# A layernorm, S5 recurrence and gated feed-forward kernel: outputs in the gate's buffers, one chunk's skip term on VectorE, and a reordered start

**Chip and metric.** One core of a Trainium2 chip. The time is the device time in microseconds (us) of one execution. "Span" is the time from the first to the last instruction in the profile; a timed execution is 1.73 to 1.86 us longer than its span in every kernel here but one (`skip_only`, 2.12 to 2.17).

## The reference

Types: bf16 in and out; L = 2048 tokens, D = 448, F = 1792.

```python
x  = A_x                                            # 1 x 2048 x 448
xn = (x - mean) / sqrt(var + 1e-5)                  # layernorm over D, no gain
Bu = xn @ B_bar^T                                   # complex, 448 states
h_t = Lam_bar * h_(t-1) + Bu_t                      # one recurrence over all tokens
s  = 2 * Re(h @ C^T) + xn * Dskip                   # "y" and the "skip"
g  = silu((silu(xn @ w_gate) * (xn @ w_up)) @ w_down)
out = x + s * g
```

## The kernel before

Tokens are worked on in four chunks (q = 0 to 3) of 512, each of four tiles (j) of 128. Per chunk: the two wide products (banks `gp`, `up`), their evacuation and product into `Vt`; `hd = Vt @ Wd` and the gate `sg = silu(hd)`; the inputs of the recurrence (`pb` banks), the scans on VectorE; `y` from the states; then the output. VectorE's scans of the next chunk run as "background" steps between its other work, so that whatever holds VectorE up early also delays everything behind it. The "root" is 1/sqrt(var) of a chunk, formed on GpSimd (`act_root`); `rcol` is a power that GpSimd forms from VectorE's `zr`, for the scans; the "iota" is GpSimd's count of the tokens (`count_tokens`). The parts that the change touches (cuts marked `# ...`):

```python
    def power(out, base, exponent):                 # GpSimd: e ** z, and 1/sqrt(var)
        powers.append(lambda: nc.gpsimd.tensor_tensor(out=out, in0=base, in1=exponent, op=ALU.pow))

    def tell(mm):                                   # a notice: a no-operation on GpSimd's queue
        told = nc.gpsimd.nop(nofuse=True)           # that waits for the matmul mm
        tc.add_manual_dep(told.ins, mm.ins.name, SYNC, reason="share")
        return told.ins.name

    def told_of(mm, notice):                        # matmul mm waits for the notice
        tc.add_manual_dep(mm.ins, notice, SYNC, reason="other half")

    def sums(q, pairs, between=None):               # two products at once, half the rows each;
        left = []                                   # the halves are exchanged after `tell`
        for share, first in ((0, True), (1, False)):
            for n, two in enumerate(pairs):
                # ... matmuls; the second share's first one waits: told_of(mm, left[n])
                if first:
                    left.append(tell(mm))
            if first:
                run_power()                         # a waiting pow goes onto GpSimd's queue here
            if first and between:
                between()

    def act_root(q):                                # 1/sqrt(var) of a chunk, on GpSimd
        # ... tensor_scalar vep <- sums ; tensor_tensor rstd <- vep ** -0.5 ; off_of <- off_of * rstd

    def down(q, j):
        # ... 14 matmuls into hd
        sg = work.tile([P, D], BF16, name="sg", bufs=TQ)
        nc.scalar.activation(sg[:], hd, ACT.Silu)
        return sg

    SKIPS = [(q, j) for q in (1, 2, 3) for j in range(TQ)][:-1]   # tiles whose skip VectorE adds

    def out_sum(q, j, k0=0, k1=KT):
        # ... seven matmuls into y, and where (q, j) is not in SKIPS also the skip term:
                nc.tensor.matmul(y[:, s + half : s + P], lhsT=xT[:, n, m * P : (m + 1) * P],
                                 rhs=Dd[:, n, half:P], start=False, stop=False)

    def finish(q, j, y, sg, eng=nc.sync, c0=0, c1=D):
        # ...
        if (q, j) in SKIPS:
            nc.vector.tensor_tensor(out=t[:], in0=y, in1=skip[q][:, j, c0:c1], op=ALU.add)
            y = t[:]
        nc.vector.tensor_tensor(out=t[:], in0=y, in1=sg[:, c0:c1], op=ALU.mult)
        ob = work.tile([P, c1 - c0], BF16, name="ob", **of)       # two buffers
        nc.vector.tensor_tensor(out=ob[:], in0=t[:], in1=x_all[:, m, c0:c1], op=ALU.add)
        eng.dma_start(out=out2d[m * P : (m + 1) * P, c0:c1], in_=ob[:])

    sg = downs(0, 1.8, {...})                       # 1.8 us of background per tile
    bg.finish(0)
    turned_norms(8, 9, 10, 11)                      # four token transposes on SyncE's queue
    outs(0, sg)                                     # and behind them the four output transfers
    sg = downs(1, 2.4, { ...
        2: act_sums((14, 15), 1) + [on(act_root, 3)],
    })
    drive(2, 4.8)
    gu(2, bg, 2.4)
    bg.finish(1)
    turned_norms(12, 13, 14, 15)
    outs(1, sg)
```

Of the kernel before, what the change touches and what calls it, by code (L numbers as in the profile page):

```python
# [44 lines left out]
def kernel(  # L45
# [187 lines left out]

    def ln_stats(n):
        st = work.tile([P, nc.vector.BN_STATS_DIM], F32, name="st")
        nc.vector.bn_stats(out=st[:], in_=x_all[:, n, :])
        nc.vector.bn_aggr(out=mv[:, n, :], in_=st[:])
        nc.vector.tensor_scalar(
            out=vep[:, n : n + 1], in0=mv[:, n, 1:2], scalar1=1e-5, scalar2=None, op0=ALU.add
        )  # L240
# [202 lines left out]

    def sums(q, pairs, between=None):

# [3 lines left out]
        for share, first in ((0, True), (1, False)):  # L449
            for n, two in enumerate(pairs):  # L450
                for m in range(4 - share):
                    for half in range(2):
                        out, w, (c0, c1) = two[half ^ share]
                        d, h = HALVES[half ^ share][share][m]
                        mm = nc.tensor.matmul(  # L455
                            out, lhsT=w[h, d, :], rhs=xT[h, d, q * W + c0 : q * W + c1],
                            start=(first and m == 0), stop=(not first and m == 3 - share),
                        )
                        if not first and m == 0:
                            told_of(mm, left[n])  # L460
                if first:
                    left.append(tell(mm))
            if first:
                run_power()
            if first and between:
                between()

# [88 lines left out]

    def gu_matmuls(q, f0, banks, *cols, **kw):

        cols = cols * (len(banks) if len(cols) == 1 else 1)
        sums(q, [  # L560
            [(to[:, c[0] : c[1]], w[:, :, block(f0 + n)], c) for to, w in zip(two, (Wg, Wu))]
            for n, (two, c) in enumerate(zip(banks, cols))
        ], **kw)

    def gu(q, bg, budget, hooks={}, begun={}):
# [3 lines left out]
        for f0 in range(0, NF, GRP):  # L569
# [3 lines left out]
            for i in range(0, n, 2):  # L573
# [3 lines left out]
                else:  # L577
                    banks = gu_banks()
                    gu_matmuls(q, fi, banks, (0, W))
                for j, (gp_, up_) in enumerate(banks):  # L580
# [12 lines left out]
    def down(q, j):  # L593

        hd = bank("hd")[:, 0:D]
        for fi in range(NF):
# [3 lines left out]
            )  # L600
        sg = work.tile([P, D], BF16, name="sg", bufs=TQ)
        nc.scalar.activation(sg[:], hd, ACT.Silu)  # L602
        return sg

    skip = {}
    SKIPS = [(q, j) for q in (1, 2, 3) for j in range(TQ)][:-1]

    def skips(q):

        skip[q] = work.tile([P, TQ, D], BF16, name="skip", tag="nz")  # L610
        for j in range(TQ):
            for c0, c1, x0 in ((0, KF * P, 0), (KF * P, D, KF * P + R)):
                nc.vector.tensor_tensor(
# [24 lines left out]
    def finish(q, j, y, sg, eng=nc.sync, c0=0, c1=D):  # L638
# [3 lines left out]
        if (q, j) in SKIPS:  # L642
            nc.vector.tensor_tensor(out=t[:], in0=y, in1=skip[q][:, j, c0:c1], op=ALU.add)
            y = t[:]
        nc.vector.tensor_tensor(out=t[:], in0=y, in1=sg[:, c0:c1], op=ALU.mult)  # L645
        of = dict(tag="scr_a") if c1 - c0 < D else {}
        ob = work.tile([P, c1 - c0], BF16, name="ob", **of)
        nc.vector.tensor_tensor(out=ob[:], in0=t[:], in1=x_all[:, m, c0:c1], op=ALU.add)  # L648
        eng.dma_start(out=out2d[m * P : (m + 1) * P, c0:c1], in_=ob[:])

# [10 lines left out]
    for n in range(2):  # L661
        ln_norm(n)
        ln_evacuate(n, ln_transpose(n), nc.scalar)
        warm(1 + n)
    for n in range(2, TQ):
        ln_stats(n)
        ln_root(n, n + 1)
    run_power()
    powers.append(count_tokens)

    def second_tokens():
        ln_evacuate(2, ln_transpose(2), nc.scalar)
        t = ln_transpose(3)
        tv = params_row(t)
        ln_evacuate(3, t, nc.vector)
        nc.scalar.activation(pcol[:], tv, ACT.Copy)
        power(dtv[:], euler[:], pcol[:, 0:KT, 0])

    CW = W // 2
    first, third = gu_banks(), gu_banks(1)  # L680
    gu_matmuls(0, 0, first, (0, CW))
    for n in range(2, TQ):
        ln_norm(n)
    gu_matmuls(0, 2, third, (0, CW), between=second_tokens)

    def first_pair():
        gu_matmuls(0, 0, first, (CW, W))
        return first

    def second_pair():  # L690
        banks = third + gu_banks(1)
        gu_matmuls(0, 2, banks, (CW, W), (0, W))
        return banks
# [67 lines left out]
    def act_sums(ns, squares):  # L761
# [3 lines left out]
    drive(1, 4.0)  # L765
    sg = downs(0, 1.8, {
        0: cw(2)[0] + cw(3)[0] + act_sums((8, 9), 0),
        1: act_sums((10, 11), 0) + [act_means] + act_sums((8, 9), 1) + cw(2)[1] + cw(3)[1],
        2: act_sums((10, 11), 1) + [on(act_root, 2), on(skips, 1)],
    })  # L770
# [3 lines left out]
    sg = downs(1, 2.4, {  # L774
        0: act_sums((12, 13, 14), 0) + [on(skips, 2)],
        1: act_sums((15,), 0) + [act_means] + act_sums((12, 13), 1),
        2: act_sums((14, 15), 1) + [on(act_root, 3)],
    })
    drive(2, 4.8)
    gu(2, bg, 2.4)  # L780
    bg.finish(1)
    turned_norms(12, 13, 14, 15)
    outs(1, sg)
    sg = downs(2, 2.4, {1: [on(skips, 3)]})
    drive(3, 4.8)
# [38 lines left out]
```

## Time and profile before

| | before |
|---|---|
| median of three timed runs (range) | 187.49 us (187.25 to 187.87) |
| the profiled run: time, span | 186.79 us, 185.0 us |
| TensorE busy | 177.9 us, 96% |
| longest wait of TensorE | 1.3 us, for Vt of the third chunk |
| longest idle of VectorE in the middle | 7.68 us, for an output transfer |

How to read the lines of the profile, here and in the prediction: a line of a timeline has start, duration, engine, line, operation, output <- inputs, sizes and count, and in brackets how long the engine stood idle before it and what ended that. A line of waits has who waited, for what, and then us in total, times, longest. "PEld" is TensorE's loading of weights, DVE VectorE, ACT ScalarE, POOL GpSimd, SP SyncE; a "q" behind the name means the engine's instruction queue.

The profile page cuts the span into 40 slices of 4.6 us and gives each engine's busy share in tenths. VectorE in the kernel before:

```profile
DVE  4649799999999999902999999999999999999583
```

The "02" in the middle is 78.6 to 87.9 us: VectorE does next to nothing there, the wait for the output tile. Everything between it and the tail is 9, so the lost time is not made up. The chain that ended last, summed by engine:

```profile
PE 67%; DVE 25%; DMA 3%; issue 2%; ACT 1%; POOL 0%; SPq 0%; DVEq 0%
```

A quarter of the path to the end runs through VectorE and a little through the DMA, although TensorE is busy 96% of the time.

### The profile page before, as it was taken

What the parts mean: (1) busy time and instruction counts of PE and PEld (TensorE: products, weight loads), DVE (VectorE), ACT (ScalarE), POOL (GpSimd) and SP (SyncE); (2) the same over time, 40 slices, a digit from 0 to 9 for tenths busy, and PEclk for the clock granted to TensorE, in tenths of its full rate; (3) what the DMA queues carried; (4) which work ended last, traced back from release to release, by engine and by line L of the source; (5) the groups of instructions that cost most, each with busy time, mean ns of one, the idle gap of its engine ahead of it and who ended that gap; (6) DMA issues with size and microseconds to landing.
All of it is one profiled execution on the core that took longest, in us unless ns stands there. A gap on an engine that the chain in (4) does not pass through costs nothing.

```text
span 185.0 us, 3723 instructions
## 1 busy us (share of the span) xinstructions
PE 177.9 (96%) x1449; PEld 87.8 (47%) x1449; DVE 160.1 (87%) x254; ACT 120.2 (65%) x247; POOL 13.4 (7%) x25
## 2 busy tenths in 40 slices
PE   7899999999999999999999999979999999999991
PEld 3574444544444555555454444535454444455551
DVE  4649799999999999902999999999999999999583
ACT  3247879997789999498499556962259696512110
POOL 7332200000000000600300000000000000000000
PEclk9999999999999999999999999999999999999999
DMA  5899655979200000043100000042100000001111
GB/s 160 209 277 338 124 94 112 132 167 377 101 0 0 5 0 0 0 86 81 50 2 4 2 0 4 0 82 70 62 4 0 0 4 0 0 4 50 50 50 50
DMA packets 26129, 12.71 MB, mean 69 GB/s; under 512 B 16000, under 2 KB 26112, under 8 KB 26112
## 3 DMA queue, kind: packets, MB, share of 16 engines
q1 hardware_dynamic: 24896, 12.06, 25.3%
q10 hardware_dynamic: 1088, 0.41, 0.8%
q8 instruction: 11, 0.18, 0.4%
q14 instruction: 6, 0.05, 0.1%
q0 software_dynamic: 128, 0.00, 0.0%
HBM read 7.23 MB, written 1.84 MB: 49 GB/s over the span
## 4 chain that ended last, share of the span: by engine, by line
PE 67%; DVE 25%; DMA 3%; issue 2%; ACT 1%; POOL 0%; SPq 0%; DVEq 0%
PE gp L455 20%; PE hd L597 16%; PE up L455 15%; PE pb L455 9%; PE y L626 7%; DVE bu_re L527 5%; DVE bu_im L527 4%; DVE tmp L521 2%; DVE Vt L589 2%; DVE ob L648 2%; DMA out_dram<-ob 2%; DVE t L645 2%; DVE H_im L521 2%; DVE ere L521 1%; DMA x_all<-in_A_x_dram 1%
## 5 line engine op out<-in xcount | busy, mean ns | idle before, releaser
L455 PE MATMUL gp<-xT,Wg 64*128 64x512 bf16 (+1 forms) x413 | 85.8, 365 | 0.4 <-ACT xT L304 0.3
L455 PE MATMUL up<-xT,Wu 64*128 64x512 bf16 (+1 forms) x413 | 85.8, 365 | 0.0
L455 PEld LDWEIGHTS <-Wg 64*128 64x128 bf16 x413 | 38.5, 94 | 25.1 <-issue 0.4
L455 PEld LDWEIGHTS <-Wu 64*128 64x128 bf16 x413 | 38.4, 94 | 19.7 <-POOLq L437 0.5
L581 ACT ACTIVATE gs<-gp 128x512 bf16<-128x512 f32 x56 | 33.7, 604 | 19.6 <-PE gp L455 11.7
L597 PE MATMUL hd<-Wd,Vt 128*128 128x448 bf16 x224 | 43.4, 353 | 1.3 <-DVE Vt L589 1.3
L585 ACT ACTIVATE us<-up 128x512 bf16<-128x512 f32 x54 | 32.9, 609 | 0.0
L597 PEld LDWEIGHTS <-Vt 128*128 128x128 bf16 x224 | 21.8, 98 | 22.0 <-DVE Vt L589 1.7
L602 ACT ACTIVATE sg<-hd 128x448 bf16<-128x448 f32 x16 | 8.6, 538 | 25.2 <-PE hd L597 20.6
L455 PE MATMUL pb<-xT,BT 64*128 64x512 bf16 (+1 forms) x224 | 21.9, 349 | 0.0
L648 DVE TENSOR_TENSOR ob<-t,x_all 128x448 bf16<-128x448 f32 (+2 forms) x17 | 10.2, 597 | 8.2 <-DMA out_dram<-ob 7.7
L589 DVE TENSOR_TENSOR Vt<-gs,us 128x2048 bf16<-128x2048 bf16 (+1 forms) x16 | 17.2, 1079 | 0.0
L455 PEld LDWEIGHTS <-BT 64*128 64x128 bf16 x224 | 10.7, 94 | 11.4 <-issue 0.7
L626 PE MATMUL y<-C,H_re 128*128 128x448 bf16 (+2 forms) x68 | 15.7, 342 | 0.0
L527 DVE TENSOR_TENSOR_SCAN bu_re<-rcol,H_re,ere 128x512 bf16<-128x512 f32 x12 | 14.9, 1262 | 0.1
L488 ACT ACTIVATE bu_re<-pb 128x512 bf16<-128x512 f32 (+1 forms) x20 | 10.1, 537 | 2.7 <-PE pb L455 2.6
L626 PE MATMUL y<-C,H_im 128*128 128x448 bf16 (+2 forms) x51 | 11.9, 342 | 0.0
L498 ACT ACTIVATE bu_im<-bu_re 64x512 bf16<-64x512 bf16 x16 | 10.0, 628 | 2.1 <-DVE bu_re L527 1.8
L527 DVE TENSOR_TENSOR_SCAN bu_im<-rcol,H_im,eim 128x512 bf16<-128x512 f32 x9 | 11.4, 1262 | 0.0
L287 ACT ACTIVATE xn<-x_all,off_of,rstd 128x384 bf16<-128x384 bf16 (+1 forms) x16 | 8.1, 588 | 2.8 <-POOL off_of L281 2.8
L521 DVE TENSOR_TENSOR tmp<-bu_im,ST 128x2048 bf16<-128x2048 bf16 x8 | 9.7, 1218 | 0.0
L626 PEld LDWEIGHTS <-H_re 128*128 128x128 bf16 x68 | 6.4, 98 | 6.1 <-issue 0.4
(98 smaller groups left out, 174.5 us busy)
## 6 DMA issues: line engine op xcount, KB each, us to landing
out_dram<-ob SPq DMA_DIRECT2D x15, 112.0 KB, 1.7
Wd<-in_B_w_down_dram SPq DMA_DIRECT2D x1, 1568.0 KB, 9.0
x_all<-in_A_x_dram SPq DMA_DIRECT2D x1, 896.0 KB, 5.5
Wg<-in_B_w_gate_dram SPq DMA_DIRECT2D x2, 384.0 KB, 7.0
Wu<-in_B_w_up_dram SPq DMA_DIRECT2D x2, 384.0 KB, 7.6
x_all<-in_A_x_dram SPq DMA_DIRECT2D x1, 448.0 KB, 5.7
Wg<-in_B_w_gate_dram SPq DMA_DIRECT2D x1, 288.0 KB, 3.1
Wu<-in_B_w_up_dram SPq DMA_DIRECT2D x1, 288.0 KB, 4.2
```

Of the source, the lines that this page charges most:

```text
L455: mm = nc.tensor.matmul(out, lhsT=w[h, d, :], rhs=xT[h, d, q * W + c0 : q * W + c1], start=(first and m == 0), stop=(not first and m == 3 ...
L488: nc.scalar.activation(to, pair[i][0], ACT.Copy)
L498: nc.scalar.activation(out[a], in_[b], ACT.Copy)
L521: nc.vector.tensor_tensor(out=of(out, n), in0=of(a, n), in1=of(b, n), op=op)
L527: nc.vector.tensor_tensor_scan(out=T["b"][c][:, k, :], data0=rcol[:, k : k + 1].to_broadcast([P, W]), data1=T["e"][c][:, k, :], initial=in ...
L581: nc.scalar.activation(gs[:, i + j, :], gp_[:], ACT.Silu)
L585: nc.scalar.activation(us[:, i + j, :], up_[:], ACT.Copy)
L589: nc.vector.tensor_tensor(out=Vt[:, f0 : f0 + n, :], in0=gs[:, 0:n, :], in1=us[:, 0:n, :], op=ALU.mult)
L597: nc.tensor.matmul(hd, lhsT=Vt_of[q][:, fi, j * P : (j + 1) * P], rhs=Wd[:, fi, :], start=(fi == 0), stop=(fi == NF - 1),)
L602: nc.scalar.activation(sg[:], hd, ACT.Silu)
L626: nc.tensor.matmul(y[:, c0:c1], lhsT=h, rhs=C2[:, n, c0:c1], start=(n == 0), stop=(n == NS - 1))
L648: nc.vector.tensor_tensor(out=ob[:], in0=t[:], in1=x_all[:, m, c0:c1], op=ALU.add)
```

## The change

Intent: take VectorE's wait away (outputs in place of the gate, so no ring of two output tiles), take the 16 skip matmuls of the first chunk from TensorE and let VectorE form the term as ((x - mean) * Dskip) * rstd + y, and start the matmuls sooner. Four parts, called A to D below. Cut to its core:

```diff
 # A: outputs in place
-        sg = work.tile([P, D], BF16, name="sg", bufs=TQ)
+        sg = work.tile([P, D], BF16, name="sg", bufs=TQ + 2)
-        ob = work.tile([P, c1 - c0], BF16, name="ob", **of)
-        nc.vector.tensor_tensor(out=ob[:], in0=t[:], in1=x_all[:, m, c0:c1], op=ALU.add)
+        ob = sg[:, c0:c1]            # (the split last tile keeps its own ob)
+        nc.vector.tensor_tensor(out=ob, in0=t[:], in1=x_all[:, m, c0:c1], op=ALU.add)
 # B: skip of chunk 0 on VectorE
-    SKIPS = [(q, j) for q in (1, 2, 3) for j in range(TQ)][:-1]
+    SKIPS = [(q, j) for q in range(NQ) for j in range(TQ)][:-1]
+            if q == 0:               # in skips(q)
+                nc.vector.scalar_tensor_tensor(
+                    out=skip[q][:, j, :], in0=x_all[:, j, :], scalar=mv[:, j, 0:1],
+                    in1=skip["row"][:], op0=ALU.subtract, op1=ALU.mult)
+                continue
-            nc.vector.tensor_tensor(out=t[:], in0=y, in1=skip[q][:, j, c0:c1], op=ALU.add)
+            nc.vector.scalar_tensor_tensor(
+                out=t[:], in0=skip[q][:, j, c0:c1], scalar=1.0 if q else rstd[:, j : j + 1],
+                in1=y, op0=ALU.mult, op1=ALU.add)
 # C: start
-        ln_evacuate(n, ln_transpose(n), nc.scalar)       # tile 1 by ScalarE alone
+    nc.scalar.activation(to[0], tps[0], ACT.Copy)        # its halves by two engines
+        nc.vector.tensor_copy(out=to[1], in_=tps[1])
-    gu_matmuls(0, 2, third, (0, CW), between=second_tokens)
+    # the left half of the third block now follows the transposes of tiles 2 and 3,
+    # and the notices are ordered anew (`since`, `gone`):
+            0, (2, third[0], left), (0, first[0], right), (1, first[1], right), since=""
-    powers.append(count_tokens)
+    count_tokens()                                       # GpSimd's iota, right away
 # D: schedule
-    sg = downs(0, 1.8, {
+    sg = downs(0, 1.3, {
-        2: act_sums((14, 15), 1) + [on(act_root, 3)],
+        2: act_sums((14, 15), 1),
     bg.finish(1)
+    act_root(3)
     turned_norms(12, 13, 14, 15)
```

More of the change, by code (lines that the diff above doesn't have):

```diff
@@ L232, with ln_stats @@
     rstd = ctile([P, NT], F32, "rstd")
-    def ln_stats(n):
+    def ln_stats(n, between=None):
         st = work.tile([P, nc.vector.BN_STATS_DIM], F32, name="st")
         nc.vector.bn_stats(out=st[:], in_=x_all[:, n, :])
+        if between:
+            between()
         nc.vector.bn_aggr(out=mv[:, n, :], in_=st[:])
@@ L442, in told_of, with sums @@
         tc.add_manual_dep(mm.ins, notice, SYNC, reason="other half")
-    def sums(q, pairs, between=None):
+    def sums(q, pairs, since=None):
         left = []
@@ L460, in sums @@
                             told_of(mm, left[n])
+                        if since and first and m == n == 0:
+                            told_of(mm, since)
                 if first:
                     left.append(tell(mm))
-            if first:
+                elif n == 0 and since == "":
+                    gone = tell(mm)
+                    run_power()
+            if first and since != "":
                 run_power()
-            if first and between:
-                between()
+        return gone if since == "" else None
     def bu(q, ns, packed=False, between=()):
@@ L555, in gu_banks, with gu_matmuls @@
         return [[bank("gp"), bank("up")] for _ in range(n)]
-    def gu_matmuls(q, f0, banks, *cols, **kw):
-        cols = cols * (len(banks) if len(cols) == 1 else 1)
-        sums(q, [
-            [(to[:, c[0] : c[1]], w[:, :, block(f0 + n)], c) for to, w in zip(two, (Wg, Wu))]
-            for n, (two, c) in enumerate(zip(banks, cols))
+    def gu_matmuls(q, *blocks, **kw):
+        return sums(q, [
+            [(to[:, c[0] : c[1]], w[:, :, block(f)], c) for to, w in zip(two, (Wg, Wu))]
+            for f, two, c in blocks
         ], **kw)
@@ L578, in gu @@
                     banks = gu_banks()
-                    gu_matmuls(q, fi, banks, (0, W))
+                    gu_matmuls(q, *((fi + n, two, (0, W)) for n, two in enumerate(banks)))
                 for j, (gp_, up_) in enumerate(banks):
@@ L605, with skip_tile @@
     skip = {}
-    SKIPS = [(q, j) for q in (1, 2, 3) for j in range(TQ)][:-1]
+    SKIPS = [(q, j) for q in range(NQ) for j in range(TQ)][:-1]
+    def skip_tile(q):
+        skip[q] = work.tile([P, TQ, D], BF16, name="skip", tag="nz")
     def skips(q):
-        skip[q] = work.tile([P, TQ, D], BF16, name="skip", tag="nz")
         for j in range(TQ):
+            if q == 0:
+                nc.vector.scalar_tensor_tensor(
+                    out=skip[q][:, j, :], in0=x_all[:, j, :], scalar=mv[:, j, 0:1],
+                    in1=skip["row"][:], op0=ALU.subtract, op1=ALU.mult,
+                )
+                continue
             for c0, c1, x0 in ((0, KF * P, 0), (KF * P, D, KF * P + R)):
@@ L642, in finish @@
         if (q, j) in SKIPS:
-            nc.vector.tensor_tensor(out=t[:], in0=y, in1=skip[q][:, j, c0:c1], op=ALU.add)
+            nc.vector.scalar_tensor_tensor(
+                out=t[:], in0=skip[q][:, j, c0:c1], scalar=1.0 if q else rstd[:, j : j + 1],
+                in1=y, op0=ALU.mult, op1=ALU.add,
+            )
             y = t[:]
         nc.vector.tensor_tensor(out=t[:], in0=y, in1=sg[:, c0:c1], op=ALU.mult)
-        of = dict(tag="scr_a") if c1 - c0 < D else {}
-        ob = work.tile([P, c1 - c0], BF16, name="ob", **of)
-        nc.vector.tensor_tensor(out=ob[:], in0=t[:], in1=x_all[:, m, c0:c1], op=ALU.add)
-        eng.dma_start(out=out2d[m * P : (m + 1) * P, c0:c1], in_=ob[:])
+        ob = sg[:, c0:c1]
+        if c1 - c0 < D:
+            ob = work.tile([P, c1 - c0], BF16, name="ob", tag="scr_a")[:]
+        nc.vector.tensor_tensor(out=ob, in0=t[:], in1=x_all[:, m, c0:c1], op=ALU.add)
+        eng.dma_start(out=out2d[m * P : (m + 1) * P, c0:c1], in_=ob)
     bg = Background()
@@ L662, with second_half @@
         ln_norm(n)
-        ln_evacuate(n, ln_transpose(n), nc.scalar)
-        warm(1 + n)
+        if n == 0:
+            ln_evacuate(n, ln_transpose(n), nc.scalar)
+            warm(1)
+    tps = [bank("tp", BF16)[:, 0 : 2 * P] for _ in range(2)]
+    for k in range(KT):
+        nc.tensor.transpose(tps[k // 2][:, block(k % 2)], xn[1][:, blk(k)], Id[:])
+    to = [xT_of(1)[:, 2 * i : 2 * i + 2, :] for i in range(2)]
+    tps = [tp.rearrange("p (k c) -> p k c", k=2) for tp in tps]
+    nc.scalar.activation(to[0], tps[0], ACT.Copy)
+    warm(2)
+    def second_half():
+        nc.vector.tensor_copy(out=to[1], in_=tps[1])
     for n in range(2, TQ):
-        ln_stats(n)
+        ln_stats(n, second_half if n == 2 else None)
         ln_root(n, n + 1)
     run_power()
-    powers.append(count_tokens)
-    def second_tokens():
-        ln_evacuate(2, ln_transpose(2), nc.scalar)
-        t = ln_transpose(3)
-        tv = params_row(t)
-        ln_evacuate(3, t, nc.vector)
-        nc.scalar.activation(pcol[:], tv, ACT.Copy)
-        power(dtv[:], euler[:], pcol[:, 0:KT, 0])
-    CW = W // 2
+    left, right = (0, W // 2), (W // 2, W)
     first, third = gu_banks(), gu_banks(1)
-    gu_matmuls(0, 0, first, (0, CW))
+    gu_matmuls(0, (0, first[0], left), (1, first[1], left))
+    count_tokens()
     for n in range(2, TQ):
         ln_norm(n)
-    gu_matmuls(0, 2, third, (0, CW), between=second_tokens)
+    t = ln_transpose(2)
+    tv = params_row(t)
+    ln_evacuate(2, t, nc.scalar)
+    nc.scalar.activation(pcol[:], tv, ACT.Copy)
+    ln_evacuate(3, ln_transpose(3), nc.vector)
+    power(dtv[:], euler[:], pcol[:, 0:KT, 0])
+    gone = []
     def first_pair():
-        gu_matmuls(0, 0, first, (CW, W))
+        gone.append(gu_matmuls(
+            0, (2, third[0], left), (0, first[0], right), (1, first[1], right), since=""
+        ))
         return first
@@ L691, in second_pair @@
         banks = third + gu_banks(1)
-        gu_matmuls(0, 2, banks, (CW, W), (0, W))
+        gu_matmuls(0, (2, banks[0], right), (3, banks[1], (0, W)), since=gone[0])
         return banks
@@ L765 @@
     drive(1, 4.0)
-    sg = downs(0, 1.8, {
+    sg = downs(0, 1.3, {
         0: cw(2)[0] + cw(3)[0] + act_sums((8, 9), 0),
         1: act_sums((10, 11), 0) + [act_means] + act_sums((8, 9), 1) + cw(2)[1] + cw(3)[1],
-        2: act_sums((10, 11), 1) + [on(act_root, 2), on(skips, 1)],
+        2: act_sums((10, 11), 1) + [on(act_root, 2), on(skip_tile, 0), on(skip_tile, 1),
+                                    on(skips, 1)],
+        3: [on(skips, 0)],
     })
@@ L774 @@
     sg = downs(1, 2.4, {
-        0: act_sums((12, 13, 14), 0) + [on(skips, 2)],
+        0: act_sums((12, 13, 14), 0) + [on(skip_tile, 2), on(skips, 2)],
         1: act_sums((15,), 0) + [act_means] + act_sums((12, 13), 1),
-        2: act_sums((14, 15), 1) + [on(act_root, 3)],
+        2: act_sums((14, 15), 1),
     })
@@ L781 @@
     bg.finish(1)
+    act_root(3)
     turned_norms(12, 13, 14, 15)
     outs(1, sg)
-    sg = downs(2, 2.4, {1: [on(skips, 3)]})
+    sg = downs(2, 2.4, {1: [on(skip_tile, 3), on(skips, 3)]})
     drive(3, 4.8)
```

## The prediction

> **What bounds the kernel now.** I read the page first, then what TensorE waited for, then the timelines of VectorE, SyncE and TensorE around those waits, and last the start. The page:
>
> ```profile
> PE 177.9 (96%) x1449; PEld 87.8 (47%) x1449; DVE 160.1 (87%) x254; ACT 120.2 (65%) x247; POOL 13.4 (7%) x25
> ```
>
> TensorE is busy in 177.9 of 185.0 us. Taking away its waits can gain 7.1 us at the very most; anything more has to come from giving it less work. What TensorE waited for:
>
> ```profile
> PE hd L597 <- DVE Vt L589: 1.3, 1, 1.3
> PE warm L179 <- DVE Wd L170: 1.1, 1, 1.1
> PE gp L455 <- ACT xT L304: 0.3, 1, 0.3
> PE tp L298 <- DVE xn L251: 0.3, 1, 0.3
> ```
>
> That is 3.0 us. Most of the rest of the 7.1 is the tail: the last matmul ends near 181.1, and VectorE's last products, the last transfer and the end of the program fill the time to 185.0. Between start and tail TensorE stops once, for 1.3 us, on the last piece of Vt of the third chunk. Why VectorE is late with it is seen 40 us earlier (VectorE's timeline, then SyncE's queue):
>
> ```profile
> 78.44 0.62 DVE L645 TENSOR_TENSOR t<-y,sg 128x448 f32<-128x448 f32 x1
> 86.74 0.63 DVE L648 TENSOR_TENSOR ob<-t,x_all 128x448 bf16<-128x448 f32 x1 [7.68 <-DMA out_dram<-ob]
> ...
> 123.86 0.68 DVE L589 TENSOR_TENSOR Vt<-gs,us 128x1024 bf16<-128x1024 bf16 x1
> ```
> ```profile
> 78.09 5.13 SPq L309 DMA_TRANSPOSE xT<-xn  x4
> 83.32 5.83 SPq L649 DMA_DIRECT2D out_dram<-ob  x4
> ```
>
> The output tile ob has two buffers. The third output of chunk 0 needs the first one's buffer back; that transfer stands in SyncE's queue behind four token transposes (78.09 to 83.2) and lands near 86.7. VectorE idles 7.68 us, and from 86.74 to 172.5 its timeline shows no other idle: it runs late all the way, and at 123.86 it is the one that TensorE waits for.
>
> The start has a second place to look at, because the page counts it as busy:
>
> ```profile
> 13.79 0.63 DVE L236 BATCH_NORM_STATS2 st<-x_all 128x6 f32<-128x448 bf16 x1 [0.39 <-DMA x_all<-in_A_x_dram]
> ...
> 16.16 0.16 DVE L344 TENSOR_TENSOR zr<-dtv,pcol 128x4 f32<-128x4 f32 x1
> ...
> 16.40 1.19 POOL L222 TENSOR_TENSOR rcol<-euler,zr 128x4 f32<-128x4 f32 x1 [3.37 <-DVE zr L344]
> 16.43 0.09 PEld L455 LDWEIGHTS <-Wu 64*128 64x128 bf16 x1 [0.52 <-POOLq L437]
> ```
>
> A weight load at 16.43 waits for a notice on GpSimd's queue. The notice stands behind the power rcol, which waits for VectorE's zr, whose chain begins when the tokens of chunk 1 land at 13.79. TensorE's pace there (0.2155 us per pair of 512-column matmuls, the pair before at 16.03) would have had it start at 16.24: 0.19 us lost.
>
> **What the Trainium skill says.** (1) "TensorE: Matmul & The Clock Gate", section "Back-to-back issue gap": 134 cycles for 128 columns, about 60 up to 64 columns, at 2.4 GHz. Three skip matmuls of 128 columns and one of 64 are then an estimated 0.19 us per tile. The trace agrees: tiles of y with skip matmuls are 1.52 us apart (72.27, 73.79), those without 1.33 (115.59, 116.93, 118.25). (2) "VectorE: DVE Perf Modes", sections on the tier table and on the fixed extra latency: two-input products with a PSUM or fp32 operand pass one element per cycle, (N+151)/0.96 ns, 624 ns for 448. The trace has 0.62 us for t and ob. For scalar_tensor_tensor the tier table has no row, so I take this trace's own: 0.68 us long, 0.69 apart, for C at L422. (3) "DMA: Bandwidth & Descriptors", section "Anatomy of one DMA": waits are served on the issuing sequencer before dispatch, and completion costs some 2 us. The trace: issue at 83.32, landing seen 3.3 us on (1.7 is the median of these transfers). (4) "PSUM — Partial Sum Buffer", section "Engine vs sequencer instructions": a no-operation only waits for what is before it to be dispatched. The trace agrees: rcol runs to 17.59, yet TensorE goes on at 16.43, just after its dispatch.
>
> **The change part by part.**
>
> *Skip of chunk 0 by VectorE.* The order of instructions loses 16 skip matmuls (12 of 128 columns, 4 of 64) where TensorE has no gap: 4 x 0.19 = 0.8 us less on the path. VectorE gets four products (4 x 0.69 = 2.8 us) and four additions to y (4 x 0.65 = 2.6 us): 5.4 us more.
>
> *Outputs in place of the gate.* The output goes into sg, which gets six buffers in place of four. The 7.7 us wait at 86.74 goes. VectorE's balance is 7.7 - 5.4 = 2.3 us. I followed the new order instruction by instruction with this trace's spacings: H of chunk 0 done at 65.1, C waits about 0.5 us for ScalarE's operands (it now comes before eim), eim, skips of chunk 1, the rest of eim, skips of chunk 0 to 75.4, ere to 76.6, four tiles at 2.0 to 84.6, skips of chunk 2 to 86.1, tmp and ere to 88.5. There the scans of chunk 1 start, which before was at 90.19: 1.7 us earlier.
>
> *Smaller budgets.* One scan (1.2) and one H_im product (0.9) move from ahead of the last Vt of chunk 2 to behind the outputs of chunk 1. From the scans to the end of that Vt was 124.46 - 90.19 = 34.3 us; less 2.1 is 32.2, so it ends near 88.5 + 32.2 = 120.7. TensorE now asks for it at 123.34 - 0.8 = 122.5. The wait of 1.26 us goes whole, with 1.8 us to spare.
>
> *Third block's left half behind the transposes.* ScalarE's and VectorE's halves of tile 1 let the first block start perhaps 0.25 us sooner, and the left half covers the evacuations. But both only bring TensorE earlier to the notice behind rcol. The tokens still land at 13.79, zr still comes at 16.2, the notice at 16.4. I count nothing for it.
>
> Sum: 0.8 + 1.26 + 0 = 2.1 us. Span 185.0 - 2.1 = 182.9; time 187.49 - 2.1 = **185.4 us**.
>
> **The rivals.** (A) *The wait moves to the gate.* sg is now free only when its output has landed. The third sg of chunk 1 takes the buffer of chunk 0's first output, which lands near 86.6 behind the same transposes, and TensorE has the tile ready at 86.5 - 0.8 = 85.7. So ScalarE waits about 0.9 us in place of VectorE's 7.7. For its costing time: ScalarE evacuates the next matmuls too. Against: before, ScalarE idled 1.8 us just afterwards for a scan, which the new order no longer asks of it there, and the banks it must free are wanted only at about 91.4. If it stalls TensorE after all, 0.5 to 1 us return: 186 to 186.4. (B) *VectorE becomes the bound*: additions and skip products slower than 0.69, or a stall I have not seen, would use up the 1.8 us in hand and keep the 1.26 us wait: 186.7. Against: both sizes are measured here. (C) *The start counts after all*: the tokens land sooner, or zr is not what holds the notice. Then up to 0.3 or 0.4 us more is gained: 185.0. Against: the next weights also land only shortly before their use (the second Wu piece of 384 KB, issued at 9.64, takes 7.6 us, to about 17.2; wanted at 17.74).
>
> **Range and chances.** The matmuls and the 1.26 us are measured sizes, and only the start and rival A move the sum by more than run-to-run spread (187.25 to 187.87). I take 184.7 to 186.5. Faster by 2% needs 183.74, or 3.75 us: more than every wait of TensorE outside start and tail together with the matmuls removed, so 0.03. Slower by 2% would need nearly 4 us of new waits: 0.01. Within 2%: 0.96.
>
> **What would show each step right or wrong.** TensorE's tiles of y of chunk 0 stand 1.33 apart, and no skip matmul is left but those of the last tile. The wait of ob for its transfer is gone, and VectorE's scans of chunk 1 begin near 88.5. TensorE's list of waits has no Vt in it. At the start, the first gp comes before 7.11, but a weight load still waits for GpSimd and starts at about 16.4. The tail, from the last chunk's first addition (174.36) to the end, keeps its 10.6 us. I am wrong if TensorE shows a new wait on ScalarE or on sg after 85, if Vt stays in the list, or if the start's gain survives past 16.4.

## The result

| | before | after |
|---|---|---|
| median (range), runs of the same rounds | 187.37 us (186.91 to 187.87), 4 runs | 184.60 us (184.30 to 185.11), 4 runs |
| span of the profiled run | 185.0 us | 182.9 us |
| TensorE busy | 177.9 us | 177.6 us |

The ratio is 0.9855, with a 95% interval of 0.982 to 0.9889. It is the mean of one kernel's runs over that of the other's in the same rounds, so not quite the ratio of these medians; all ratios below are formed so. The predicted span (182.9) came; the predicted time, 185.4 us, and its range, from 184.7, did not.

The page of the kernel after, its VectorE slices and its chain:

```profile
PE 177.6 (97%) x1433; PEld 87.2 (48%) x1433; DVE 165.5 (91%) x263; ACT 119.8 (65%) x247; POOL 15.0 (8%) x25
...
DVE  4749799999999989989999999999999999999583
...
PE 89%; DVE 7%; DMA 1%; POOL 1%; issue 1%; DVEq 0%
```

The hole in VectorE's row is filled, and VectorE's part of the chain has fallen from 25% to 7%: the end now hangs on TensorE nearly throughout. Sixteen matmuls are gone (1449 to 1433). The busy sum hardly shows it, as overlapping matmuls are not counted twice; the positions of the tiles do. TensorE before, the first and second tile of y in chunk 0:

```profile
72.27 0.35 PE L626 MATMUL y<-C,H_re 128*128 128x448 bf16 x1
72.46 0.22 PE L632 MATMUL y<-Dd,xT 128*128 128x128 bf16 x1
...
73.79 0.35 PE L626 MATMUL y<-C,H_re 128*128 128x448 bf16 x1
```

And after, all four:

```profile
72.34 0.92 PE L641 MATMUL y<-C,H_re 128*128 128x448 bf16 x4
...
73.67 0.92 PE L641 MATMUL y<-C,H_re 128*128 128x448 bf16 x4
...
74.99 0.92 PE L641 MATMUL y<-C,H_re 128*128 128x448 bf16 x4
...
76.32 0.92 PE L641 MATMUL y<-C,H_re 128*128 128x448 bf16 x4
```

The pitch falls from 1.52 to 1.33 us, four times 0.19. VectorE's timeline after:

```profile
72.70 2.47 DVE L622 SCALAR_TENSOR_TENSOR skip<-x_all,mv,skip_row 128x448 bf16<-128x448 bf16 x4
...
76.22 0.67 DVE L658 SCALAR_TENSOR_TENSOR t<-skip,rstd,y 128x448 f32<-128x448 bf16 x1
...
81.93 0.62 DVE L667 TENSOR_TENSOR sg<-t,x_all 128x448 bf16<-128x448 f32 x1
...
88.64 2.46 DVE L534 TENSOR_TENSOR_SCAN bu_re<-rcol,H_re,ere 128x512 bf16<-128x512 f32 x2
...
120.03 0.67 DVE L595 TENSOR_TENSOR Vt<-gs,us 128x1024 bf16<-128x1024 bf16 x1
```

The third output (81.93) follows without idle where before VectorE stood for 7.68 us. The skip products cost 2.47 us for four, the additions with a pointer scalar 0.67. The scans of chunk 1 begin at 88.64 (predicted 88.5), and the last Vt of chunk 2 ends at 120.7 (predicted 120.7), before TensorE asks. TensorE's waits of the kernel after, besides the 1.1 us of the warm-up at the very start, are one line, and Vt is not in it:

```profile
PE tp L300 <- DVE xn L253: 0.2, 1, 0.2
```

The start, GpSimd and the weight loads after (the prediction shows the same place of before):

```profile
16.47 1.19 POOL L222 TENSOR_TENSOR rcol<-euler,zr 128x4 f32<-128x4 f32 x1 [3.40 <-PE up L458]
...
16.50 0.09 PEld L458 LDWEIGHTS <-Wu 64*128 64x128 bf16 x1 [0.55 <-POOLq L439]
```

The first `gp` came at 6.90 in place of 7.11, yet TensorE still stops for the notice behind rcol and goes on at 16.51, against 16.43 before. The tail begins at

```profile
172.21 0.62 DVE L658 SCALAR_TENSOR_TENSOR t<-skip,y 128x448 f32<-128x448 bf16 x1 [1.69 <-PE y L641]
```

and lasts to 182.9, 10.7 us (10.6 before). So in the profiled pair of executions every step is as written: 0.8 + 1.26 + 0. What needs explaining is why the medians differ by 2.8 us in these rounds, and whether each part did what it was credited with.

### The profile page after: what moved, and what is told of

Same layout as the page of the kernel before. It is cut to its first block, busy times and chain, and to the rows that moved or that the text cites. A ratio compares the mean times of both kernels' runs of the same rounds, so it can differ in the third digit from the quotient of the medians.

```text
span 182.9 us, 3701 instructions
## 1 busy us (share of the span) xinstructions
PE 177.6 (97%) x1433; PEld 87.2 (48%) x1433; DVE 165.5 (91%) x263; ACT 119.8 (65%) x247; POOL 15.0 (8%) x25
## 4 chain that ended last, share of the span: by engine, by line
PE 89%; DVE 7%; DMA 1%; POOL 1%; issue 1%; DVEq 0%
PE gp L458 26%; PE hd L603 22%; PE up L458 20%; PE pb L458 12%; PE y L641 10%; DVE t L663 1%; DVE st L236 1%; DMA x_all<-in_A_x_dram 1%; DVE t L658 1%; DVE sg L667 1%; POOL rstd L222 1%; DVE xn L253 1%; DVE ob L667 0%; DVE mv L239 0%; DVE vep L240 0%
## 5 line engine op out<-in xcount | busy, mean ns | idle before, releaser
L458 PEld LDWEIGHTS <-BT 64*128 64x128 bf16 x224 | 10.7, 94 | 11.4 <-issue 0.7
L641 PE MATMUL y<-C,H_re 128*128 128x448 bf16 (+2 forms) x68 | 15.1, 342 | 0.0
L663 DVE TENSOR_TENSOR t<-t,sg 128x448 f32<-128x448 f32 x15 | 9.4, 625 | 0.9
L667 DVE TENSOR_TENSOR sg<-t,x_all 128x448 bf16<-128x448 f32 x15 | 9.4, 625 | 0.5
```

Source lines behind the costliest of these rows:

```text
L458: mm = nc.tensor.matmul(out, lhsT=w[h, d, :], rhs=xT[h, d, q * W + c0 : q * W + c1], start=(first and m == 0), stop=(not first and m == 3 ...
L641: nc.tensor.matmul(y[:, c0:c1], lhsT=h, rhs=C2[:, n, c0:c1], start=(n == 0), stop=(n == NS - 1))
L667: nc.vector.tensor_tensor(out=ob, in0=t[:], in1=x_all[:, m, c0:c1], op=ALU.add)
```

## The experiments

Theory S: the sizes in the sum are right, and the base was wrong, as the executions behind the median of 187.49 were longer than the profiled one, by waits that the change takes away. Rival T: a part of the change (start C, or the schedule D) is worth more than it was given. Rival K: it is only the chip, a clock or a session, and the difference is 2.1 us when both are run often. All kernels gave correct results. Ratios are of fast runs against before's in the same rounds of one session; the single looks, one run each, are of unknown state and are read by their profiles. (A fifth idea, four output tiles instead of outputs in place, only got as far as a build: the work buffers would need 82.8 KB a partition where 81.2 are left.)

### First session: both again, and A and B apart

Before: 187.0 us (11 runs, 186.62 to 187.39). The two controls have no edit.

> The kernel before, unchanged. The prediction gave the span of the profiled run right (182.9 us) but the time 0.8 us too long: it took 2.1 us from the median of the timed runs (187.49), while the profiled run of before took 186.79. Theory S: executions of before differ by some 0.7 us, because its late VectorE passes every delay on to TensorE's wait for Vt, so its typical execution waits nearer 2 us than 1.26. Then this profile shows a wait for Vt of 1.5 to 2.2 us and a span of 185.3 to 186.1 at clock 1.0. Theory K: the longer executions have a granted clock a few thousandths below 1; then they differ in clock and not in the wait. Theory P: taking the profile shortens the run; then all profiled runs lie some 0.7 us below their timed ones.

Measured: 186.93 us, ratio 0.9998 (0.998 to 1.0017), span 185.2, mean granted clock 0.995.

> The changed kernel, unchanged: 184.6 us, ratio 0.985. Theory S: its runs spread less than those of before, and no wait for Vt shows. Theory K: its longer runs have a clock below 1. Theory P: its profiled run lies below its timed ones too.

Measured: 184.79 us (184.25 to 185.26), ratio 0.9879 (0.9859 to 0.9899), span 182.5. The medians are 2.2 us apart here, not 2.8, and 0.9879 is close to the predicted 185.4/187.49 = 0.9888. The smaller spread that was expected did not show (1.0 us, against 0.8 of the 11 runs of before beside it). Theory P falls: the profiled execution is one of the six timed ones, here the fastest, in `root_back` below the slowest. In the span of the control before, the wait for Vt is larger than in the profile that was predicted from:

```profile
PE hd L597 <- DVE Vt L589: 1.6, 1, 1.6
```

`inplace_only` is part A on the kernel before and nothing else:

```diff
-        sg = work.tile([P, D], BF16, name="sg", bufs=TQ)
+        sg = work.tile([P, D], BF16, name="sg", bufs=TQ + 2)
-        nc.vector.tensor_tensor(out=ob[:], in0=t[:], in1=x_all[:, m, c0:c1], op=ALU.add)
+        nc.vector.tensor_tensor(out=ob, in0=t[:], in1=x_all[:, m, c0:c1], op=ALU.add)   # ob = sg[:, c0:c1]
```

> The kernel before with the output written into the gate sg (six buffers) and nothing else. By the prediction's steps the 7.7 us wait of VectorE goes, the wait of TensorE for Vt goes, and the 16 skip matmuls stay: span 185.0 - 1.26 = 183.7, ratio 0.993. Theory S: also what before loses in its typical runs comes back, so the ratio is nearer 0.989. Rival A (the wait moves to sg): a wait of sg for the transfer of its first output of about 0.9 us, and if it costs, ratio 0.995 to 0.998.

Measured: 186.31 us, ratio 0.9963 (0.9948 to 0.9977), span 184.3. Less than expected. Its waits of TensorE:

```profile
PE pb L455 <- POOLq L437: 0.8, 1, 0.8
```

Vt is gone from the list, and a wait for GpSimd's queue is there in its place. GpSimd's timeline, then TensorE's:

```profile
88.59 0.84 POOL L274 TENSOR_SCALAR vep<-sums_of 128x4 f32<-128x4 f32 x1 [11.90 <-ACT junk L263]
89.51 1.91 POOL L278 TENSOR_TENSOR rstd<-vep,halves 128x4 f32<-128x4 f32 x1
91.49 0.20 POOL L281 TENSOR_TENSOR off_of<-off_of,rstd 128x4 f32<-128x4 f32 x1
```
```profile
91.53 3.75 PE L455 MATMUL pb<-xT,BT 64*128 64x512 bf16 x40 [0.83 <-POOLq L437]
```

The three instructions of chunk 3's root stand on GpSimd's queue in front of the notice that the second share of a `pb` pair needs. The last of them is sent off at 91.49, and TensorE goes on at 91.53. In the kernel before the same three stand there too, but were through in time; its power took half as long:

```profile
88.92 1.01 POOL L278 TENSOR_TENSOR rstd<-vep,halves 128x4 f32<-128x4 f32 x1
```

The prediction's rival A, a wait of the gate for its buffer, is also there, but only 0.28 us long, and it held nothing up that TensorE listed.

`skip_only` is B and D without A and C (so the output ring of two stays):

```diff
-        ob = sg[:, c0:c1]
+        ob = work.tile([P, c1 - c0], BF16, name="ob", **of)   # and bufs=TQ again; the start as before
```

> The changed kernel with its old start and with two ob buffers again (sg has four): skip of chunk 0 by VectorE, the smaller budget and the moved root alone. 0.8 us of matmuls go, but VectorE has 5.4 us more and still waits for the buffer of ob to about 87, so its scans of chunk 1 start near 94 in place of 90.2, and 2.1 us of work moved behind the last Vt don't make up for it: TensorE waits some 3.7 us for Vt, span 186.5 to 187, ratio 1.005 to 1.012. If VectorE's lateness is not what makes the wait, the ratio is 0.995.

Measured: 187.04 us, ratio 1.0007 (0.9991 to 1.0023), span 184.9. VectorE's timeline:

```profile
81.00 0.63 DVE L659 TENSOR_TENSOR t<-t,sg 128x448 f32<-128x448 f32 x1
85.67 0.63 DVE L662 TENSOR_TENSOR ob<-t,x_all 128x448 bf16<-128x448 f32 x1 [4.05 <-DMA out_dram<-ob]
...
92.39 1.28 DVE L529 TENSOR_TENSOR_SCAN bu_re<-rcol,H_re,ere 128x512 bf16<-128x512 f32 x1
```

```profile
PE hd L599 <- DVE Vt L591: 2.0, 1, 2.0
```

TensorE's wait for Vt was 2.0 us, not the expected 3.7: the transfer landed 1.96 us after its issue at 83.71, earlier than the 86.7 to 87 that I had carried over from before. The size was too pessimistic, the direction right: most of the 0.8 us of matmuls that TensorE saves comes back as a longer wait for VectorE (2.0 us, against 1.26 to 1.57 in the profiles of before). By spans B without A still gains some 0.3 us (medians 184.9 and 185.2); in device time that is lost, because this kernel spends 2.12 to 2.17 us outside its span, every other kernel here 1.73 to 1.86. Why it does was not found. A pays for B.

### Second session: what the moved root and the start are worth

Before: 187.1 us (11 runs). `inplace_root` is A and the moved root, `root_back` the whole change with the root put back, `no_start` the whole change with the start of before.

```diff
 # inplace_root, on inplace_only             (root_back, on after: these lines the other way)
-        2: act_sums((14, 15), 1) + [on(act_root, 3)],
+        2: act_sums((14, 15), 1),
     bg.finish(1)
+    act_root(3)
```

> The run inplace_only (output in the gate on the kernel before) lost part of its gain: TensorE waited 0.83 us at a matmul of chunk 2 for a notice on GpSimd's queue, where the root of chunk 3 stood in front of it, waiting for squares of ScalarE that came after an sg delayed by its transfer. This kernel is inplace_only with that root moved behind the third chunk's gate, as the change does. If that account is right the wait is gone, TensorE has no wait for Vt either, span 183.4 to 183.8 against 184.3, ratio about 0.992. If the rival holds that the output in place simply gains less, the ratio stays at 0.996.

Measured: 185.37 us (185.13 to 185.39), ratio 0.9901 (0.9878 to 0.9924), span 183.6. TensorE lists no wait but the warm-up's, and its `pb` matmuls run through (56 without a stop, where inplace_only shows 16 and, after the wait, 40):

```profile
89.07 5.47 PE L455 MATMUL pb<-xT,BT 64*128 64x512 bf16 x56
```

> The changed kernel with the root of chunk 3 back where it was. By the same account TensorE again waits 0.5 to 1.3 us for GpSimd's queue in the matmuls of chunk 2, span 183.2 to 183.8, ratio to before about 0.992 against 0.988 for the whole change. If the root's place does not matter here, the ratio stays at 0.988.

Measured: 185.56 us, ratio 0.9914 (0.9894 to 0.9935), span 184.1. Two waits of TensorE are in it:

```profile
PE up L458 <- POOLq L439: 0.7, 1, 0.7
PE pb L458 <- POOLq L439: 0.6, 1, 0.6
```

The second is the root again, so it costs 0.6 to 0.8 us wherever it is left in its old place and VectorE no longer waits. The account of it, squares that come late after a delayed gate, is not the main part: here no gate waits for a transfer, yet TensorE does. The power itself took 1.98 us here and 1.91 in inplace_only, beside VectorE's scans, against 1.01 in the profile of before, where VectorE was still at its skip products; these 0.9 us alone are more than either wait. That it is the scans that slow it was not isolated. The first is the start: the tokens of chunk 1 landed at 14.36 in this execution rather than 13.79, zr came at 16.73, and TensorE went on at 17.00 rather than 16.5. The start's notice is a wait that differs from one execution to the next.

```diff
 # no_start, on after
-    gu_matmuls(0, (0, first[0], left), (1, first[1], left))
+    gu_matmuls(0, 0, first, (0, CW))
-            0, (2, third[0], left), (0, first[0], right), (1, first[1], right), since=""
+    gu_matmuls(0, 2, third, (0, CW), between=second_tokens)      # and the rest of C undone
```

> The changed kernel with its old start. The prediction counted nothing for the new start because a notice behind rcol holds TensorE at about 16.4; in four of six profiles so far that wait isn't there at all, yet counted from the first normalization the new start has TensorE only 0.07 us ahead at 16. So: slower than the whole change by 0.0 to 0.1 us, ratio to before 0.988. If the start is worth what its parts seem to say (0.3 us), ratio 0.990.

Measured: 184.54 us, ratio 0.9859 (0.9836 to 0.9883), span 182.7: nothing lost with the start undone. The whole change was not run beside these three (0.9879 and 0.9877 in the other two), but the traces agree: TensorE's first y comes at 72.02 to 72.75 us in the eleven profiles with the old start and at 71.98 to 72.84 in the five with the new one. Rival T falls for C. The same rounds also measure B alone: no_start is inplace_root with B and the smaller budget, and 185.37 less 184.54 is 0.83 us. A profile more of before:

> The kernel before once more, for its profile alone. Theory S (the wait for Vt varies with the landing of chunk 0's first output, and passes one for one): the two profiles so far have landing seen 3.4 and 3.8 us after the issue and waits of 1.26 and 1.6. Here the wait for Vt is again the landing's delay less about 2.2, within 0.15.

Measured: 186.96 us, span 185.2, wait for Vt 1.44 us, the landing (3.59) less 2.15.

### Third session: the notice, the iota and the budget

Before: 186.9 us (11 runs). Two questions: whether C could have gained, and whether the smaller budget of D mattered. `late_rcol` moves rcol one pair of notices later; `late_both` does so and also moves the iota (`count_tokens`) behind the first notices; `budget_18` puts 1.8 back.

```diff
 # late_both, on after            (late_rcol: only the run_power line)
-            if first and since != "":
+            if first and since == "":
+                count_tokens()
+            if first and since is None:
                 run_power()
-    count_tokens()               # after the first gu_matmuls
 # budget_18, on after
-    sg = downs(0, 1.3, {
+    sg = downs(0, 1.8, {
```

> The changed kernel once more, to compare the next ones with on one chip: ratio to before 0.985 to 0.989, spans 182.4 to 183.4, no wait for Vt.

Measured: 184.82 us (184.29 to 185.03), ratio 0.9877 (0.9853 to 0.99), span 182.6.

> The changed kernel with rcol alone moved by one pair. It never waits at 16.4 for GpSimd's queue. Mean gain over after_third 0.1 us (0.2 in some executions, none in most); no lower best time.

Measured: 184.53 us (184.27 to 184.77), ratio 0.9866 (0.9842 to 0.989), 0.3 us below after_third in the median.

> The changed kernel with two steps of GpSimd moved: the count of tokens (iota) to behind the first notices of the next pair, because VectorE's normalization took 0.62 us beside it in place of 0.40, and rcol by one pair, so that no notice stands behind it. By the theory of the start, TensorE no longer waits for GpSimd's queue whenever the tokens of chunk 1 land late (0.2 us in two profiles, 0.66 in a third, none in others), and the first right half starts 0.2 us sooner: span 0.2 to 0.4 us below after_third, ratio 0.984 to 0.987, and less spread. If the weights that land at 17.2 hold TensorE instead, nothing is gained.

Measured: 184.20 us (184.01 to 184.38), ratio 0.9848 (0.9825 to 0.9872), span 182.4: the fastest kernel, ahead of both. Its VectorE and GpSimd lines at the start, after those of the kernel after:

```profile
8.83 0.62 DVE L253 TENSOR_SCALAR xn<-x_all,mv,rstd 128x448 bf16<-128x448 bf16 x1 [0.44 <-POOL rstd L222]
```
```profile
8.76 0.56 POOL L212 IOTA it_f<- 128x512 f32 x1
```
```profile
8.87 0.40 DVE L253 TENSOR_SCALAR xn<-x_all,mv,rstd 128x448 bf16<-128x448 bf16 x1 [0.44 <-POOL rstd L222]
```
```profile
11.47 0.56 POOL L212 IOTA it_f<- 128x512 f32 x1 [2.63 <-PE up L458]
```

In the kernel after, the fourth tile's normalization runs beside GpSimd's iota and takes 0.62 us in place of 0.40, and TensorE is waiting for that tile. The Trainium skill, page "SBUF — State Buffer", section "Who interferes with whom", says that a tensor_scalar in a mode that uses both ports shares one pair with GpSimd, and that whoever comes first blocks the other for the whole of its instruction. The trace agrees that the two disturb one another (0.62 against 0.40); a block until the iota's end at 9.32 would have put the end of xn near 9.7, and it came at 9.45, but GpSimd's spans are rough. VectorE's products t of 448 columns also take 0.62 us in these traces, so it may have run at a slower pace rather than stood still; no run tells the two apart.

> The changed kernel with the background budget of the first chunk's gate products at 1.8 again, as before. VectorE then does some 1 to 2 us more of scans ahead of the last Vt of chunk 2, which ended 1.8 us before TensorE asked for it. By the ledger the wait for Vt stays away or is at most 0.4 us: ratio 0 to 0.002 above after_third. If VectorE's order matters more than its sum, a wait of 1 us or more comes back.

Measured: 184.85 us, ratio 0.9889 (0.9864 to 0.9914), span 182.9, and no wait for Vt among TensorE's. Its last Vt of chunk 2:

```profile
121.74 0.68 DVE L595 TENSOR_TENSOR Vt<-gs,us 128x1024 bf16<-128x1024 bf16 x1
```

That ends at 122.4, just in time (a weight load waited 0.2 us for it). The budget only adds reserve.

### Fourth session: four more profiles of before

What was still open was what a long execution of before has in it. The edit is none.

> The kernel before, for its profile: executions of it spread from 184.7 to 186.5 us in span, and the three profiles so far all fell between 185.0 and 185.2. Theory S: a longer span comes with a longer wait for Vt (1.3 to 1.6 so far), at 185.6 about 1.9, and the wait is the landing of chunk 0's first output after its issue, less 2.2 us. Theory T: it comes with a later landing of tokens at the start (the first normalization at 4.7, or the weight load that waits for GpSimd near 16.4), with the wait for Vt unchanged or shorter. Theory K: a clock of 0.995 alone.

> As look_1: S, a span over 185.4 goes with a wait for Vt over 1.7; T, with a late start; K, with the clock.

> As look_1: S, a span over 185.4 goes with a wait for Vt over 1.7; T, with a late start; K, with the clock.

> As look_1: S, a span over 185.4 goes with a wait for Vt over 1.7; T, with a late start; K, with the clock.

Measured, beside the three profiles of before that were there already (all in us; "landing" is from SyncE's issue of the first output of chunk 0 to when VectorE goes on):

| profile of before | span | TensorE at the first y | at chunk 2's first hd, 2.4 us before the wait | landing | wait for Vt |
|---|---|---|---|---|---|
| the one predicted from | 185.0 | 72.27 | 120.90 | 3.42 | 1.26 |
| before_again | 185.2 | 72.06 | 120.76 | 3.80 | 1.57 |
| before_look | 185.2 | 72.23 | 120.86 | 3.59 | 1.44 |
| look_1 | 185.8 | 72.30 | 121.38 | 4.17 | 1.57 |
| look_2 | 184.9 | 72.19 | 120.82 | 3.42 | 1.26 |
| look_3 | 185.8 | 72.75 | 121.40 | 3.72 | 1.57 |
| look_4 | 185.1 | 72.31 | 120.94 | 3.42 | 1.26 |

In each row the span is 185.0, plus the difference in where y starts, plus that in the stretch from y to hd, plus that in the wait, within 0.1: the tail behind is the same. VectorE's wait in look_2 (short) and look_1 (long):

```profile
86.66 0.63 DVE L648 TENSOR_TENSOR ob<-t,x_all 128x448 bf16<-128x448 f32 x1 [7.68 <-DMA out_dram<-ob]
```
```profile
87.53 0.63 DVE L648 TENSOR_TENSOR ob<-t,x_all 128x448 bf16<-128x448 f32 x1 [8.43 <-DMA out_dram<-ob]
```

When the transfer lands later, VectorE is later, and so TensorE's wait 40 us on is longer: it is the landing less about 2.2 us. In look_1 0.45 us of the delay reach TensorE sooner, between y and hd. Its scan is 0.75 us later there, ScalarE waits 2.56 us for it in place of 1.81, and so empties the `pb` banks later; TensorE's weight loads for the next gate products stand still until just after it has done so (the profile names no releaser, the times fit):

```profile
94.07 0.59 ACT L488 ACTIVATE bu_im<-pb 128x512 bf16<-128x512 f32 x1
94.71 0.09 PEld L455 LDWEIGHTS <-Wg 64*128 64x128 bf16 x1 [0.34 <-issue]
```

So the landing passes one for one in all seven rows, within 0.03 us: what it is over 3.42 equals what the stretch from y to hd and the wait have gained together (0.75 = 0.45 + 0.31 in look_1). look_3 was late already at y, and its list of waits has the start's notice in it:

```profile
PE up L455 <- POOLq L437: 0.3, 1, 0.3
```

Theory S thus missed in its number, a wait over 1.7 us with a span over 185.4: both long executions waited 1.57, no more than before_again at 185.2. It is right on the cause for look_1, whose 0.8 us are all the landing's; look_3 owes 0.3 us to the landing and the rest to its start (theory T of the expectation above).

The clock does not sort them: look_2 is the shortest at a mean granted clock of 0.996. Rival K in its form "a slower clock" falls.

## Why the prediction was right or wrong

**The mechanism and the sizes for the profiled execution were right.** The skip matmuls gave 0.8 us (1.52 to 1.33 a tile), the Vt wait of 1.26 us went whole, the start gave nothing, the tail kept its length, and the span came out at the predicted 182.9 us. The experiments add up with the same terms if each profile's span is counted from TensorE's first y of chunk 0, which leaves the start out. Before: 185.0 - 72.27 = 112.7 us, and 111.5 without the 1.26 of wait; inplace_root has 183.6 - 72.30 = 111.3. Less 0.8 is 110.7; the change has 182.9 - 72.34 = 110.6 and no_start 182.7 - 72.17 = 110.5. With the waits that they show, inplace_only should have 111.5 + 0.83 = 112.3, and has 184.3 - 72.02 = 112.3; skip_only should have 110.7 + 2.0 = 112.7, and has 184.9 - 72.07 = 112.8.

**The step that failed** is the second half of "Span 185.0 - 2.1 = 182.9; time 187.49 - 2.1 = 185.4 us": its base, not its 2.1. The profiled run took 186.79 us; 187.49 is the median of three longer ones. In the later sessions, with 11 runs of before each, the medians of before are 187.0, 187.1 and 186.9. Where the change was timed beside them, 187.0 - 2.1 = 184.9 stands against 184.79 measured, and 186.9 - 2.1 = 184.8 against 184.82. So of the miss of 0.8 us some 0.5 is a base of three runs that came out long, and 0.2 are four runs of the change that came out short (184.60). Rival K in its second form, a difference of 2.1 us when both are run often, holds: the medians differ by 2.2 and 2.1 us there, beside 2.8 in the first rounds. Whether session, chip or chance made those first runs of before long is not known. Had I put the 1.79 us between time and span of the profiled run onto 182.9, the answer would have been 184.7 us; that this one run lies so near the later medians is luck.

What makes one execution of before longer than another is in part a wait that the change removes. The landing behind the term "1.26" is 3.42 us in three of seven profiles and up to 4.17 in the rest (mean 3.65), and passes one for one, so before loses on average 0.23 us more by it than I counted. The change's last Vt is ready at 120.7 with 1.8 us to spare, so this goes too; it is too little for the miss of 0.8. The start's notice cost look_3 0.45 us at y (against look_1 and look_4, whose first gp comes at the same 7.34). The four executions of before behind 187.37 were not profiled, so what they lost stays open.

**The range** was too narrow at its lower end. I took run-to-run spread from three runs of before (0.6 us). The change itself scatters from 184.25 to 185.26, and of its 16 timed runs 8 lie below 184.7.

**"VectorE's balance is 7.7 - 5.4 = 2.3 us"** and the new order held: the products were cheaper than estimated (0.62 against 0.69 each), the tiles of chunk 0 stood 2.09 to 2.18 apart against 2.0, and the two nearly cancel: scans at 88.64 against 88.5. That they cancel is luck.

**Rival A** was wrong as I put it. In the kernel after, the gate shows no wait for its transfer. A relative was real: with VectorE early, chunk 3's root on GpSimd stood in front of TensorE's notices for 0.6 to 0.8 us, unless it is moved, and the change moves it. I read that hunk of the diff and gave it no value, so my account of A holds only with it (0.9963 without the move, 0.9901 with it, each against before in its own session).

**Rival B** did not come; budget_18 shows that even the reserve of 1.8 us could be cut to about nothing. **Rival C**, a start that counts, did not either (no_start 0.9859). The step "both only bring TensorE earlier to the notice behind rcol" is true of the profiled execution; I had not seen a second hold-up, the iota beside the last normalization. Moving rcol and the iota took the median from 184.82 to 184.20 us in one session, 0.3 of it with rcol alone. In the two profiles the first y is only 0.14 us sooner (71.94 against 72.08), and the same moves were not tried on the old start, so that it is the new start that gains by them is not shown.

## What to carry to other kernels

Before a predicted gain is taken off a measured time, ask how many runs that time stands on: here the median of three was 0.4 to 0.6 us above the medians of 11, a quarter of the whole effect. A wait that ends with a transfer has a spread, so profile the kernel before more than once. When an engine becomes earlier, look at what other queues carry in front of the notices that the waiting engine depends on: the next hold-up may be an instruction on an engine that is 8% busy.

## What the Trainium skill lacked or had wrong

- "VectorE: DVE Perf Modes", section "The perf-mode tier table": no row for scalar_tensor_tensor. The runs show 0.62 us for 448 columns with one operand in PSUM and an immediate scalar, 0.67 to 0.68 with a pointer scalar, and 2.47 us for a row of four with bf16 operands in SBUF and a pointer scalar.
- "PSUM — Partial Sum Buffer", section "Engine vs sequencer instructions": that a no-operation waits only for dispatch agrees with the runs. It calls GpSimd's queue strictly first in, first out, but does not spell out what follows for a notice: an engine instruction in front of it that waits for a third engine holds it too. This cost TensorE 0.2 to 0.8 us here.
- "SBUF — State Buffer", section "Who interferes with whom": it has two ratios of slowing, but no sizes for these instructions. The runs show the normalization at 0.62 us beside GpSimd's iota and 0.40 without it, and the root's pow of 128x4 values at 1.01 to 1.31 us beside VectorE's skip products in before, at 1.86 to 1.98 beside its scans, and at 1.32 to 2.46 beside its products before the first outputs; what slows it was not isolated.
- "DMA: Bandwidth & Descriptors", section "Anatomy of one DMA": its 2 us of fixed cost is given for transfers that GpSimd issues; SyncE's output transfers of 112 KB here have a median of 1.7 us in all. It has nothing on the first transfer behind four transposes, which took 3.4 to 4.2 us in seven profiles of before and 1.96 in skip_only; why they differ was not found.
